# Storing turned groups from another queue, and turning the first batch's through DRAM as well

## The chip, the cores and the metric

The kernel runs on one core of a Trainium2 chip. The metric is the device time of one execution in microseconds. The time before is the median of three executions.

## The reference

Three stages are computed in float32, one after another, for 4 batches of 448 tokens:

```python
scores = scale * q @ k.T - log(S)          # 12 heads of 64, S = 448
x = sigmoid(scores) @ v                    # 1792 tokens x 768
g = (x @ w_a) * (x @ w_b)                  # 1792 x 1536
y = g @ w_out                              # 1792 x 768
logits = y @ phi                           # 1792 x 32
d = softmax(logits, over tokens)
slot_input = d.T @ y                       # 32 x 768, 8 experts of 4 rows
slot_out[e] = relu(slot_input[e] @ w1[e]) @ w2[e]
out = softmax(logits, over slots) @ slot_out
```

`w1` and `w2` are 25 MB each. The softmax over tokens runs over all 1792 tokens, so the experts can begin only after the last batch.

## The kernel before

The kernel keeps `g` transposed: `gT[b, fc]` is a tile of 128 features by 448 tokens, with 12 tiles (`fc`) for each batch `b`. It never forms `y`: it folds `w_out @ phi` into `wphi` for the logits, and computes `(d.T @ g) @ w_out` for the slots. For `d.T @ g` the tiles must be turned so that tokens lie on partitions. `group(b, gi)` turns four tiles at a time (three groups to a batch), and `dg` multiplies the turned groups by the softmax weights, adding up in `acc`.

The order of the work is written out by hand, with generators. `ab(0)` multiplies the first batch by `w_a` and `w_b` on TensorE (12 blocks of 36 matmuls), each matmul in three rounded parts. Between its steps the attention of the second batch goes on, VectorE, ScalarE and GpSimd convert the raw weights (`stage0`, `stage1`: loads at L330 and L333, converted weights stored to DRAM at L370), and `fill_step` moves one step of the waiting list `fill`, in which the groups stand. Batches 1 and 2 are computed together in `unit` with fewer products. `ab(3)` then does the last batch; its weights come back from DRAM by `load_w` (L454), are rounded on VectorE (L462) and GpSimd (L463), and are multiplied at L568. Only two half tiles of the buffer `wr` serve the last loads, so a load may start when the GpSimd instruction that reads its half is done. While `ab(3)` runs, `pump` (L982) loads the first expert weights into tiles that are free. The last group and logits (`last_LG`) follow, and then the experts, whose weights stream through the ring of tiles.

There are two ways to turn a group:

- by TensorE, in 16 transposes of 128x128 (L532) whose results are copied from PSUM alternately by ScalarE and VectorE (L534). All of batch 0, and the group `gi == 2` of the others, go that way.
- by VectorE, in four instructions that transpose blocks of 32x32 (L515). `store_gk` writes the half-turned tile to the DRAM buffer `gk32` in four transfers of 224 KB (L549), and `reload_gk` reads it back in the order that `dg` needs, in two transfers (L554, L555). The groups 0 and 1 of batches 1, 2 and 3 go that way.

All these transfers are issued on the queue of SyncE (SP), which takes its instructions in order and stops at one whose inputs are not there. For batch 3 the two turned tiles are kept in the list `turned_3` and stored together at step 57 of the 72 of `ab(3)`; steps 63 and 65 reload them. ScalarE's part in `ab(3)` is one copy out of PSUM for each block (L575); it also issues two small stores of logits (L852).

Of the kernel before, what the change touches and what calls it, by code (L numbers as in the profile page):

```python
# [9 lines left out]
F32 = mybir.dt.float32  # L10
# [8 lines left out]
B, H, S, D = 4, 12, 448, 64  # L19
# [16 lines left out]
def body(ctx, tc, q, k, v, w_a, w_b, w_out, phi, w1, w2, out):  # L36
    nc = tc.nc
    pe, act, dve, pool, sp = nc.tensor, nc.scalar, nc.vector, nc.gpsimd, nc.sync
# [12 lines left out]
    drp = ctx.enter_context(tc.tile_pool(name="drp", bufs=1, space=bass.MemoryType.DRAM))  # L51
# [12 lines left out]
    def ms(shape=(128, S)):  # L64
        tags = banks[run["banks"]]
        tag = tags[run["ms"] % len(tags)]
        run["ms"] += 1
        return ps_tile(tag, list(shape), 4 if tag == "sc" else 2)
# [8 lines left out]
    gk_01 = lgp.tile([128, 2, 2048], F32, name="gk_01")  # L77
# [11 lines left out]
    ab32 = drp.tile([KF, 2, 128, KD * 128], F32, name="ab32")  # L89
    out32 = drp.tile([128, KF, DM], F32, name="out32")  # L90
    clog32 = drp.tile([T, C, B, NS], F32, name="clog32")
    gk32 = drp.tile([B - 1, 2, S, 512], F32, name="gk32")

    idj = ident.rearrange("p (j s) -> p j s", j=4)
    small = gk_01.rearrange("p a n -> p (a n)")
# [204 lines left out]
    def att_to(cost):  # L300

        while att_state[0] < cost:
            n = next(att_g, None)
            if n is None:
                return
            att_state[0] += n

    def att_pairs(n):

        while (n - 1) not in xt:  # L310
            att_state[0] += next(att_g)
# [176 lines left out]
    def project(b, gi, n):  # L488

        t, r = ms(), 32 * n  # L490
        for j in range(n):
            fc = 4 * gi + j
            pe.matmul(t[32 * j:32 * j + 32], wphi[:, fc], gT[b, fc], start=True, stop=True)  # L493
        if gi == 0:
            act.copy(lp[b], t)
        else:
            dve.tensor_tensor(lp[b][:r], lp[b][:r], t[:r], op=ALU.add)

    def group(b, gi, evac=(act.copy, dve.tensor_copy) * 2):

        if (b, gi) != (B - 1, 2):
            for _ in range(GDEL):
                yield
        if (b, gi) != (B - 1, 2):
            project(b, gi, 4)
        if (b, gi) == (B - 1, 2):
            gk = e2.tile([128, 2048], F32, tag="e20", name="gk_3")
        elif b in (1, 2):
            gk = gk_01[:, b - 1]
        else:  # L510
            gk = gk_01[:, gi] if gi < 2 else gk_2
        if b and gi < 2:
            turned = gk[:, :4 * S].rearrange("p (n f) -> p n f", f=128)
            for j in range(4):
                dve.transpose(turned[:, :, 32 * j:32 * j + 32], gT[b, 4 * gi + j].rearrange("p (n t) -> p n t", t=32))  # L515
                yield
                if b < B - 1:
                    yield
                gT.pop((b, 4 * gi + j))
                live.discard(b * KF + 4 * gi + j)  # L520
            if b < B - 1:
                store_gk(b, gi, turned)
            else:
                turned_3.append(turned)
            return
        gk = gk.rearrange("p (c n) -> p c n", c=C)
        if gi == 2 and not b:
            yield
        for c in range(C):
            tp = ms((128, 512))  # L530
            for i in range(4):
                pe.transpose(tp[:, i * 128:(i + 1) * 128],  # L532
                             gT[b, 4 * gi + i][:, STARTS[c]:STARTS[c] + 128], ident)
            evac[c](gk[:, c], tp)  # L534
            if c != 1 or (b, gi) == (B - 1, 2):
                yield
                if b < B - 1 and c < C - 1:
                    yield
        for i in range(4):
            gT.pop((b, 4 * gi + i))  # L540
            live.discard(b * KF + 4 * gi + i)
        gtok[b, gi] = gk

    turned_3 = []

    def store_gk(b, gi, turned):
        dst = gk32[b - 1, gi].rearrange("(n t) (r f) -> r t n f", t=32, r=4)
        for r in range(4):
            sp.dma_start(out=dst[r], in_=turned[32 * r:32 * r + 32])  # L549

    def reload_gk(b, gi, t):
        t = t.rearrange("p (c n) -> p c n", c=C)
        src = gk32[b - 1, gi]
        sp.dma_start(out=t[:, :3], in_=src[:384].rearrange("(c p) n -> p c n", c=3))  # L554
        sp.dma_start(out=t[64:, 3], in_=src[384:])  # L555
        gtok[b, gi] = t
# [261 lines left out]
    def tokens(src, dst):  # L818

        t = ms((T, C, NS))  # L820
        for c in range(C):
            pe.transpose(t[:, c], src[:NS, c * T:(c + 1) * T], ident[:NS, :NS])
        dve.tensor_copy(dst, t)

    def weights(d, dst):
        t = ms((128, C, NS))
        for c in range(C):
            pe.transpose(t[:, c], d[:NS, STARTS[c]:STARTS[c] + 128], ident[:NS, :NS])
        dve.tensor_copy(dst, t)

    def dg(b, dtok, gp, groups):

        kept = not b or groups[0] == 2
        gk = gtok[b, groups[0]][:, None] if len(groups) == 1 else gk_01.rearrange("p g (c n) -> p g c n", c=C)
        o = gp.rearrange("p (g n) -> p g n", g=3)[:, groups[0]:groups[-1] + 1]
        for c in range(C):
            rows = slice(64 * (c == C - 1), 128)
            for j in range(4):
                pe.matmul(o[32 * j:32 * j + 32], dtok[rows, c], gk[rows, :, c, j * 128:(j + 1) * 128] if kept  # L839
                          else gk[rows, 0, c].rearrange("p (r j f) -> p j r f", r=4, j=4)[:, j],  # L840
                          start=(c == 0), stop=(c == C - 1))

    def LG(b):
        t = run["lsd2"]
        run["lsd"] = t[:, :S], t[:, S:2 * S]
        dtok, ltok = (t[:, i:i + C * NS].rearrange("p (c s) -> p c s", c=C) for i in (2 * S, 2 * S + C * NS))
        yield
        yield from logits(b)
        run["lg"] = b
        yield  # L850
        tokens(run["lsd"][0], ltok[:T])
        (act if b else sp).dma_start(out=clog32[:, :, b], in_=ltok[:T])  # L852
        yield
        weights(run["lsd"][1], dtok)
        for _ in range(4 if b == 1 else 1):
            yield
        gp = ms((128, FF // 4))
        for groups in ((0,), (1,), (2,)) if b else ((0, 1), (2,)):
            dg(b, dtok, gp, groups)
        if b:  # L860
            dve.scalar_tensor_tensor(acc, acc, run["al"], gp, op0=ALU.mult, op1=ALU.add)
        else:
            dve.tensor_copy(acc, gp)
        yield
        if b == B - 3:
            open_slots(run["e1"], [2, 3])
        elif b == B - 2:
            run.pop("lsd2")
            open_slots(run["e1"], [1, 4, 5])
# [83 lines left out]
    def open_slots(pl, names):  # L953
        slots.extend((pl, f"{pl.name}{i}") for i in names)
# [52 lines left out]
        next(bg)  # L1007

    base = att_state[0]
    for frac in ab(0):  # L1010
        att_to(base + NP * PAIR * min(1.0, frac * 1.02))
    att_pairs(2 * NP)
    for kk in range(NP):
        xt.pop(kk)
# [44 lines left out]
    for i, frac in enumerate(ab(B - 1)):  # L1059
        fc = i // 6  # L1060
        if i < 6:
            fill_step()
        if i == 6:
            while fill:
                fill_step()
            cp_ctx.close()
            xb_ctx.close()
            e1 = run["e1"] = ctx.enter_context(tc.tile_pool(name="e1", bufs=1, side="right"))
            run["lsd2"] = e1.tile([128, 2048], F32, tag="e11", name="lsd2")
            run["wr"] = e1.tile([128, 2048], F32, tag="e10", name="wr")  # L1070
            load_w(LAST + 6)
            load_w(LAST + 7)
            for x in range(4):
                nm = f"e1{2 + x}"
                reload_gk(1 + x // 2, x % 2, e1.tile([128, 2048], F32, tag=nm, name=nm))
            open_slots(e1, range(6, NE1))
            fill.append(LG(1))
            fill.append(LG(2))
        elif i == 57:
            for gi, t in enumerate(turned_3):  # L1080
                store_gk(B - 1, gi, t)
        elif i in (63, 65):
            reload_gk(B - 1, (i - 63) // 2, gk_01[:, (i - 63) // 2])
        if i == 66:
            dve.tensor_copy(wphi[:, :4], wphi[:, KF - 1:].to_broadcast([128, 4, NS]))
        if i >= 12 and i % 3 == 0:
            pump()
# [20 lines left out]
    for what in order0:  # L1108
        i = what[1]
        h, n, f0 = (0, 4, 4 * i) if i < 3 else (1, 6, 6 * (i - 3))  # L1110
# [8 lines left out]
    for kk in range(0, KD, 2):  # L1119
        f = ms((128, 2, 256))  # L1120
# [22 lines left out]
    for kk in range(0, KE, 2):  # L1143
        f = ms((128, 2, 256))
# [37 lines left out]
    for h, (c0, w) in enumerate(COLS):  # L1182
# [4 lines left out]
        t = ms((128, w))  # L1187
        pe.matmul(t, selF.rearrange("p j s -> p (j s)"), s4[:, c0:c0 + w], start=True, stop=True)
        evac[h](s4r[:, c0:c0 + w], t)
        for c in range(C):  # L1190
            op = []
            for b in range(B):
# [3 lines left out]
                r = slice(32 * b, 32 * b + 32)  # L1196
# [32 lines left out]
```

## Time and profile before

| | |
|---|---|
| median of 3 executions | 688.71 us (687.13 to 690.76) |
| the profiled execution | 689.2 us |
| its span from the first instruction to the last | 687.4 us |
| TensorE (PE) busy | 642.6 us, 93% |
| VectorE (DVE) busy | 396.4 us, 58% |
| ScalarE (ACT) busy | 296.1 us, 43% |
| GpSimd (POOL) busy | 309.6 us, 45% |
| mean granted TensorE clock | 0.983 of full speed |
| HBM read / written | 124.53 MB / 25.34 MB |

The busy times are those of the whole span. `ab(0)` lies between about 55 and 214 us, `ab(3)` between about 457 and 573 us, and the experts begin at about 584 us. In the rows, SPq and ACTq are the queues on which these engines issue transfers. A row names what an instruction writes and reads: `gk<-gk` at L549 is a store of a turned tile, `wr<-ab` a load of weights for the last batch, `e<-in_moe_w` a load of expert weights. In brackets stands how long the engine was idle before, and what ended that.

### The profile page before, as it was taken

The numbers are of one execution on the slowest core, as the hardware profiler recorded it, in microseconds if no ns is written. First come the engines' busy times: TensorE is split into PE (matmuls) and PEld (weight loads), VectorE is DVE, ScalarE is ACT, GpSimd is POOL, SyncE is SP. The second block draws the span as 40 slices with busy tenths as digits, with TensorE's granted clock in tenths as the row PEclk, the third lists the DMA queues.
The fourth block names the chain that finished last, engine by engine and source line by source line (L and its number), as shares of the span: only waits on it lengthen the run. The fifth ranks groups of instructions, "written<-read, shape, count | busy, mean of one in ns | idle before, by whom it ended". The sixth has DMA issues, their size and how long they took to land.

```text
span 687.4 us, 10893 instructions
## 1 busy us (share of the span) xinstructions
PE 642.6 (93%) x4035; PEld 457.4 (67%) x4035; DVE 396.4 (58%) x561; ACT 296.1 (43%) x535; POOL 309.6 (45%) x236
## 2 busy tenths in 40 slices
PE   6999999999999899999999999999999968997683
PEld 4557778777676455578988988888879856442132
DVE  4676898899895468849887777744232312200022
ACT  4888779678663768863332322212100002110021
POOL 0243667667762219639996575533335422000000
PEclk9999999999999999999999999999999989999998
DMA  8998999989845356111124424233999898999998
GB/s 197 262 282 210 288 300 324 275 250 336 223 159 141 70 93 113 32 43 46 47 75 119 101 91 100 76 117 115 340 371 338 329 314 305 409 416 415 408 357 277
DMA packets 145620, 150.58 MB, mean 219 GB/s; under 512 B 81600, under 2 KB 122912, under 8 KB 142496
## 3 DMA queue, kind: packets, MB, share of 16 engines
q1 hardware_dynamic: 144640, 149.78, 69.6%
q8 instruction: 32, 0.52, 0.3%
q10 hardware_dynamic: 928, 0.11, 0.1%
q14 instruction: 20, 0.16, 0.1%
HBM read 124.53 MB, written 25.34 MB: 218 GB/s over the span
## 4 chain that ended last, share of the span: by engine, by line
PE 76%; DMA 13%; ACT 2%; DVE 2%; issue 2%; SPq 2%; POOL 1%; DVEq 0%; ACTq 0%
PE ab L568 23%; PE sc L748 15%; DMA e<-in_moe_w 8%; PE ab L748 8%; PE sc L208 6%; PE sc L221 5%; PE ms L221 4%; DMA wr<-ab 2%; PE ms L170 2%; DMA qn<-in_q 2%; PE ms L839 1%; PE ab L208 1%; DMA gkp<-in_moe_w 1%; PE ms L493 1%; SPq L549 1%
## 5 line engine op out<-in xcount | busy, mean ns | idle before, releaser
L367 POOL TENSOR_TENSOR w<-gk,cy 128x768 int32<-128x768 int32 x36 | 66.2, 1838 | 91.9 <-DVE gk L362 56.2
L211 ACT ACTIVATE a<-sc,sums 112x448 f32<-112x448 f32 x147 | 84.4, 644 | 13.0 <-PE sc L208 12.8
L568 PE MATMUL ab<-t,wh 128*128 128x448 f32 x288 | 67.3, 380 | 5.6 <-DVE wh L462 5.6
L568 PEld LDWEIGHTS ab<-t,wh 128*128 128x128 f32 x288 | 54.9, 194 | 12.3 <-issue 7.3
L463 POOL TENSOR_TENSOR wl<-wr,wh 128x768 fp32r<-128x768 f32 x16 | 29.4, 1839 | 56.6 <-DVE wh L462 32.5
L575 ACT COPY misc<-ab 128x448 f32<-128x448 f32 x24 | 12.8, 535 | 88.7 <-PE ab L568 88.7
L463 POOL TENSOR_TENSOR wl<-w,wh 128x768 fp32r<-128x768 f32 x24 | 45.5, 1899 | 2.5 <-ACT wh L462 2.5
L1160 PE MATMUL ab<-e,gk 128*32 128x384 f32 x240 | 33.4, 530 | 10.1 <-DMA e<-in_moe_w 10.1
L360 DVE TENSOR_SCALAR mf<-gk 128x768 f32<-128x768 f32 x36 | 34.0, 945 | 13.3 <-ACT gk L349 13.3
L221 PE MATMUL sc<-a,vn 112*64 112x448 f32 x192 | 39.1, 546 | 1.0 <-ACT a L211 1.0
L221 PE MATMUL ms<-a,vn 112*64 112x448 f32 x192 | 38.7, 545 | 0.5 <-ACT a L211 0.5
L578 DVE TENSOR_TENSOR misc<-misc,ab 128x448 f32<-128x448 f32 x24 | 14.8, 615 | 36.9 <-PE ab L568 36.9
L208 PE MATMUL sc<-qh,kh 64*112 64x448 f32 x147 | 34.8, 424 | 0.7 <-ACT qh L158 0.6
L361 DVE TENSOR_SCALAR gk<-mf 128x768 uint32<-128x768 uint32 x36 | 34.3, 953 | 1.2
L568 PE MATMUL ab<-xh,wh 128*128 128x448 f32 x144 | 34.9, 377 | 0.0
L568 PE MATMUL ab<-xl,wh 128*128 128x448 f32 x144 | 34.5, 375 | 0.0
L568 PE MATMUL ab<-xh,wl 128*128 128x448 f32 x144 | 34.4, 374 | 0.0
L568 PE MATMUL ab<-t,wl 128*128 128x448 f32 x144 | 34.3, 373 | 0.0
L632 POOL TENSOR_TENSOR wx<-wr,wx 128x384 fp32r<-128x384 f32 x29 | 32.3, 1116 | 3.5 <-ACT wx L631 3.4
L631 ACT CAST wx<-T 128x384 fp32r<-128x384 f32 x21 | 10.8, 513 | 53.5 <-DVE T L653 33.9
L632 POOL TENSOR_TENSOR wx<-T,wx 128x384 fp32r<-128x384 f32 x23 | 24.8, 1080 | 17.0 <-ACT wx L631 15.7
L1199 DVE COPY o<-sc 112x384 f32<-112x384 f32 x11 | 5.6, 550 | 45.7 <-PE sc L1197 45.6
(458 smaller groups left out, 1521.3 us busy)
## 6 DMA issues: line engine op xcount, KB each, us to landing
e<-in_moe_w SPq DMA_DIRECT2D x23, 1024.0 KB, 7.8
e<-in_moe_w SPq DMA_DIRECT2D x23, 768.0 KB, 15.1
wr<-ab SPq DMA_DIRECT2D x14, 768.0 KB, 4.4
ab<-w SPq DMA_DIRECT2D x24, 384.0 KB, 7.2
vn<-in_v SPq DMA_DIRECT2D x24, 224.0 KB, 4.0
gk<-gk SPq DMA_DIRECT2D x24, 224.0 KB, 4.2
e<-in_moe_w SPq DMA_DIRECT2D x14, 384.0 KB, 8.6
wr_cv<-in_moe_w_a SPq DMA_DIRECT2D x6, 768.0 KB, 7.4
```

The source lines that it names most:

```text
L208: pe.matmul(sc[h], kx[r, cs], qx[r], start=(i == 0), stop=(i == 2))
L211: act.activation(a, sc[h], AF.Sigmoid, bias=nlog[:T], scale=1.0 / math.sqrt(D))
L221: pe.matmul(pv_t[g][64 * h:64 * h + 64], qkv_t["v", g][:, h, c, :], a_t.pop((g, h, c)), start=(c == 0), stop=(c == C - 1))
L360: dve.tensor_scalar(mf, m, LOW, HIGH, op0=ALU.max, op1=ALU.min)
L361: dve.tensor_scalar(mi, mf.bitcast(U32), 3, 0x3FFFFFFF, op0=ALU.logical_shift_left, op1=ALU.bitwise_and)
L367: pool.tensor_tensor(thirds(w), m.bitcast(I32), thirds(cy_t.pop(x)), op=ALU.add)
L463: pool.tensor_tensor(wl, t, wh.bitcast(F32), op=ALU.subtract)
L568: pe.matmul(t, w[:, kk * 128:(kk + 1) * 128], xt[b * NP + kk][xi], start=(s == 0 and kk == 0), stop=(s == 2 and kk == KD - 1))
L578: dve.tensor_tensor(g, g, t, op=ALU.mult)
L632: pool.tensor_tensor(w[:, 1], t, w[:, 0].bitcast(F32), op=ALU.subtract)
L748: pe.matmul(t, w[:, wi, k * 128:(k + 1) * 128], xs[ORDER[m], k][xi], start=(s == 0 and k == 0), stop=(s == 2 and k == 2))
L1160: pe.matmul(sps[h][32 * j:32 * j + 32], hT[:, 2 * x + i, 2 * j + g], ring[order2[n + j]][0][:, i, c0:c0 + w], start=(g == 0 and x == 0 and ...
```

## The change

Two things are changed, and a third follows from them.

- Batch 3: the stores of a turned group are issued by ScalarE, right after the group has been turned, with one `yield` (one call of `fill_step`) behind each. The list `turned_3` and the stores at step 57 on SP are gone. The reloads stay on SP at steps 63 and 65.
- Batch 0: its groups 0 and 1 are turned by VectorE, stored by SP as soon as they are turned, and reloaded by SP at steps 54 and 71 of `ab(0)`. Their 32 transposes on TensorE and 8 copies out of PSUM are gone.
- `dg` multiplies batch 0's groups one at a time, each with 16 matmuls of 128 columns, as it does for the other batches. Before, the first two went together with 256 columns.

```diff
@@ group(b, gi)
-        if b and gi < 2:
+        if gi < 2:
             turned = gk[:, :4 * S].rearrange("p (n f) -> p n f", f=128)
...
-            if b < B - 1:
-                store_gk(b, gi, turned)
-            else:
-                turned_3.append(turned)
+            yield from store_gk(b, gi, turned)
             return
...
     def store_gk(b, gi, turned):
-        dst = gk32[b - 1, gi].rearrange("(n t) (r f) -> r t n f", t=32, r=4)
+        dst = gk32[b, gi].rearrange("(n t) (r f) -> r t n f", t=32, r=4)
         for r in range(4):
-            sp.dma_start(out=dst[r], in_=turned[32 * r:32 * r + 32])
+            (act if b == B - 1 else sp).dma_start(out=dst[r], in_=turned[32 * r:32 * r + 32])
+            if b == B - 1:
+                yield
@@ dg
-        kept = not b or groups[0] == 2
+        kept = groups[0] == 2
@@ LG(b)
-        for groups in ((0,), (1,), (2,)) if b else ((0, 1), (2,)):
+        for groups in ((0,), (1,), (2,)):
@@ the loop over ab(0)
-    for frac in ab(0):
+    for i, frac in enumerate(ab(0)):
         att_to(base + NP * PAIR * min(1.0, frac * 1.02))
+        if i in (54, 71):
+            reload_gk(0, i // 60, gk_01[:, i // 60])
@@ the loop over ab(B - 1)
-        elif i == 57:
-            for gi, t in enumerate(turned_3):
-                store_gk(B - 1, gi, t)
```

The first place where the instructions move is SP's queue in the second half of `ab(3)`, from one load of expert weights (tile e14) to the reloads. Before:

```order
L982 DMA e14_5721<-in_moe2_w1 128x2048
L454 DMA wr_5115<-ab32_99 128x768
L549 DMA gk32_102<-gk_01_93 32x14x128 x8
L982 DMA e15_5756<-in_moe2_w1 128x2048
L454 DMA wr_5115<-ab32_99 128x768
L982 DMA gkp0_5783<-in_moe2_w1 128x2048
L454 DMA wr_5115<-ab32_99 128x768
L554 DMA gk_01_93<-gk32_102 128x3x512
```

The same place in the changed kernel:

```order
L979 DMA e14_5714<-in_moe2_w1 128x2048
L454 DMA wr_5103<-ab32_99 128x768
L979 DMA e15_5744<-in_moe2_w1 128x2048
L454 DMA wr_5103<-ab32_99 128x768
L979 DMA gkp0_5771<-in_moe2_w1 128x2048
L454 DMA wr_5103<-ab32_99 128x768
L551 DMA gk_01_93<-gk32_102 128x3x512
```

The eight stores that stood ahead of the last two loads of weights (`wr`) have left this queue, and nothing else in it has moved.

The second place is ScalarE in `ab(3)`, with the semaphores that each instruction waits for (DMAHW is that of an earlier transfer). Before there were only the copies out of PSUM here; the changed kernel has:

```order
L544 DMA gk32_102<-gk_01_93 32x14x128 [waits DMAHW2_49,DVE_49]
L572 COPY misc_95<-ab_5477 128x448 [waits PE_49]
L544 DMA gk32_102<-gk_01_93 32x14x128 [waits DMAHW5_49]
L544 DMA gk32_102<-gk_01_93 32x14x128 [waits DMAHW0_49]
L544 DMA gk32_102<-gk_01_93 32x14x128 [waits DMAHW2_49]
L572 COPY misc_95<-ab_5536 128x448 [waits PE_49]
L572 COPY misc_95<-ab_5590 128x448 [waits PE_49]
L572 COPY misc_95<-ab_5643 128x448 [waits PE_49]
L544 DMA gk32_102<-gk_01_93 32x14x128 [waits DMAHW2_49,DVE_49]
L544 DMA gk32_102<-gk_01_93 32x14x128 [waits DMAHW4_49]
L544 DMA gk32_102<-gk_01_93 32x14x128 [waits DMAHW6_49]
L572 COPY misc_95<-ab_5707 128x448 [waits PE_49]
```

Seven of the eight stores are in these rows; up to three now stand between two copies, and each waits for an earlier transfer to land.

The third place is VectorE in `ab(0)`, where the first group of batch 0 is turned (`mf` and `gk_2` are the conversion of the raw weights). Before:

```order
L534 COPY gk_01_93<-ms_1469 128x512
L578 TENSOR_TENSOR misc_95<-misc_95,ab_1441 128x448
L158 CAST kh_1505<-ms_1495 128x448
L159 TENSOR_TENSOR kl_1506<-ms_1495,kh_1505 128x448
L360 TENSOR_SCALAR mf_1516<-gk_2_94 128x768
L361 TENSOR_SCALAR gk_2_94<-mf_1516 128x3x256
L362 SCALAR_TENSOR_TENSOR gk_2_94<-wr_cv_98,gk_2_94 128x3x256
L534 COPY gk_01_93<-ms_1556 128x512
```

In the changed kernel:

```order
L515 STREAM_TRANSPOSE gk_01_93<-misc_95 128x14x32
L575 TENSOR_TENSOR misc_95<-misc_95,ab_1436 128x448
L158 CAST kh_1489<-ms_1479 128x448
L159 TENSOR_TENSOR kl_1490<-ms_1479,kh_1489 128x448
L360 TENSOR_SCALAR mf_1500<-gk_2_94 128x768
L361 TENSOR_SCALAR gk_2_94<-mf_1500 128x3x256
L362 SCALAR_TENSOR_TENSOR gk_2_94<-wr_cv_98,gk_2_94 128x3x256
L515 STREAM_TRANSPOSE gk_01_93<-misc_95 128x14x32
```

Transposes stand where the copies stood, and two more of them lie outside these rows, so that each of the two groups has four instead of two.

## Rows read from the trace of the kernel before

**Rows 1.** Chain of work that ended last, 537 to 580 us: start, us, what.

```profile
547.43 1.25 SPq L549
...
555.45 7.08 DMA wr<-ab
```

**Rows 2.** Timeline of all engines, 545 to 571 us: start, us, instruction, idle before.

```profile
546.44 7.42 SPq L549 DMA_DIRECT2D gk<-gk  x8
546.63 0.53 ACT L575 COPY misc<-ab 128x448 f32<-128x448 f32 x1 [6.91 <-PE ab L568]
...
547.42 1.85 POOL L463 TENSOR_TENSOR wl<-wr,wh 128x768 fp32r<-128x768 f32 x1 [1.39 <-DVE wh L462]
...
551.64 1.83 POOL L463 TENSOR_TENSOR wl<-wr,wh 128x768 fp32r<-128x768 f32 x1 [2.37 <-DVE wh L462]
...
553.87 2.64 PE L568 MATMUL ab<-t,wh 128*128 128x448 f32 x12
...
555.45 0.80 SPq L454 DMA_DIRECT2D wr<-ab  x1
...
556.35 1.40 PE L568 MATMUL ab<-t,wl 128*128 128x448 f32 x6
556.86 1.41 SPq L454 DMA_DIRECT2D wr<-ab  x1
...
562.64 0.56 DVE L462 CAST wh<-wr 128x768 fp32r<-128x768 f32 x1 [11.14 <-DMA wr<-ab]
...
563.35 4.82 PE L568 MATMUL ab<-t,wh 128*128 128x448 f32 x12 [5.60 <-DVE wh L462]
566.46 0.56 DVE L462 CAST wh<-wr 128x768 fp32r<-128x768 f32 x1 [2.72 <-DMA wr<-ab]
```

**Rows 3.** Windows: us, busy of PE, PEld, DVE, ACT, POOL, PEclk, DMA share, GB/s.

```profile
510.00:520.00 10.00, 10.00 (x50) 9.08 (x49) 4.14 (x6) 0.53 (x1) 3.69 (x2) 1.00 0.79 301
540.00:590.00 50.00, 41.80 (x307) 32.37 (x307) 10.71 (x25) 5.41 (x12) 13.83 (x19) 0.93 0.90 308
563.00:568.00 5.00, 4.65 (x13) 4.15 (x14) 1.43 (x4) 0.00 (x0) 2.68 (x2) 0.50 1.03 360
590.00:650.00 60.00, 50.44 (x386) 19.00 (x385) 5.85 (x10) 4.10 (x7) 0.00 (x0) 0.94 1.02 416
```

**Rows 4.** Issues of DMA, 500 to 600 us: count, KB each, median us to landing.

```profile
e<-in_moe_w SPq DMA_DIRECT2D x23, 1024.0 KB, 7.8
wr<-ab SPq DMA_DIRECT2D x8, 384.0 KB, 4.9
```

**Rows 5.** Timeline of VectorE, 511 to 516 us, the first turned group's last transpose.

```profile
513.68 0.63 DVE L515 STREAM_TRANSPOSE gk<-misc 128x448 f32<-128x448 f32 x1
```

**Rows 6.** Timeline of TensorE in the first product, 109 to 130 us.

```profile
117.28 1.03 PE L532 MATMUL ms<-ident,misc 128*128 128x128 f32 x8
118.07 1.46 PE L568 MATMUL ab<-xh,wl 128*128 128x448 f32 x6
```

**Rows 7.** Waits of TensorE, 100 to 213 us: us in total, times, longest.

```profile
PE ms L532 <- ACT wT L393: 0.5, 2, 0.2
PE ms L532 <- DVE kl L159: 0.3, 1, 0.3
```

**Rows 8.** Chain of work that ended last, 237 to 243 and 484 to 506 us: `dg`.

```profile
238.55 3.14 PE ms L839 x64
...
485.97 3.43 PE ms L839 x96
```

**Rows 9.** Lines L515 and L534: ns of one, shortest/median/longest.

```profile
L515 DVE STREAM_TRANSPOSE gk<-misc x16: 600/632/639, 358.0 to 540.4; 128x448 f32<-128x448 f32 x16
L534 DVE COPY gk<-ms x10: 681/690/693, 120.9 to 472.0; 128x512 f32<-128x512 f32 x10
```

**Rows 10.** Windows, columns as in rows 3, the first product's busiest stretch on VectorE.

```profile
150.00:180.00 30.00, 29.25 (x178) 21.95 (x177) 28.31 (x31) 21.51 (x34) 21.91 (x12) 1.00 0.98 314
```

**Rows 11.** Waits of SP's queue, 100 to 200 us: us in total, times, longest.

```profile
SPq L330 <- DVE gk L362: 10.9, 4, 3.7
```

More of the change, by code (lines that the diff above doesn't have):

```diff
@@ L91, in body @@
     clog32 = drp.tile([T, C, B, NS], F32, name="clog32")
-    gk32 = drp.tile([B - 1, 2, S, 512], F32, name="gk32")
+    gk32 = drp.tile([B, 2, S, 512], F32, name="gk32")
     idj = ident.rearrange("p (j s) -> p j s", j=4)
@@ L542, in group @@
         gtok[b, gi] = gk
-    turned_3 = []
     def store_gk(b, gi, turned):
-        dst = gk32[b - 1, gi].rearrange("(n t) (r f) -> r t n f", t=32, r=4)
+        dst = gk32[b, gi].rearrange("(n t) (r f) -> r t n f", t=32, r=4)
         for r in range(4):
-            sp.dma_start(out=dst[r], in_=turned[32 * r:32 * r + 32])
+            (act if b == B - 1 else sp).dma_start(out=dst[r], in_=turned[32 * r:32 * r + 32])
+            if b == B - 1:
+                yield
     def reload_gk(b, gi, t):
         t = t.rearrange("p (c n) -> p c n", c=C)
-        src = gk32[b - 1, gi]
+        src = gk32[b, gi]
         sp.dma_start(out=t[:, :3], in_=src[:384].rearrange("(c p) n -> p c n", c=3))
```

## The prediction

> **What bounds the kernel now.** I read the chain of waits first. It is TensorE's work nearly everywhere, and the place where it leaves TensorE late in the last batch's product is the one that this change touches: there it runs through the stores of the turned groups on SP's queue and then through one load of weights [rows 1]. The timeline of that stretch says how. SP begins the eight stores at 546.44 and is busy with them for 7.42 us. The half tile that the next load needs is free when GpSimd's subtraction ends, at 547.42 + 1.85 = 549.27; the load is issued at 555.45, 6.2 us late. The one after it could start at 551.64 + 1.83 = 553.47 and is issued at 556.86, 3.4 us late. The weights of the first are rounded only at 562.64. TensorE has used up what it had at 556.35 + 1.40 = 557.75 and starts again at 563.35, after 5.60 us with nothing to do [rows 2]. When it does start, its granted clock is 0.50 of full speed, the 1.2 GHz level, until about 568 [rows 3]: the same twelve matmuls take 4.82 us where they took 2.64 just before [rows 2].
>
> The windows behind that place say whether time saved there is saved at the end. From 590 to 650 the DMA engines are busy throughout and move 416 GB/s: this is the stream of expert weights, bound by bandwidth, and it starts when TensorE has used the first of the loaded tiles. Between 540 and 590 their share is 0.90 [rows 3].
>
> For the first batch I read TensorE's timeline in the first product and then the engines that could hold it up. TensorE goes from one matmul to the next with waits of some 0.3 us, and VectorE is busy for 28.31 of 30 us in the tightest stretch [rows 6, 7, 10].
>
> **A. The last batch's stores leave SP's queue.** Gone is the wait of 5.60 us. Gone with it is the slow clock behind it, 4.82 - 2.64 = 2.18 us, since TensorE went into the wait at full speed and fell only there. Together 7.78 us.
>
> Does something else hold the two loads? If they take as long to land as before, the first is rounded at 549.27 + (562.64 - 555.45) + 0.56 = 557.02, ahead of the 557.75 at which TensorE wants it. The second took 566.46 - 556.86 = 9.60 us; it would be ready at 553.47 + 9.60 + 0.56 = 563.63. TensorE wants it one block of 18 matmuls later, at 557.75 + (557.75 - 553.87) = 561.63, so it would wait 2.0 us. With the median of these loads, 4.9 us, it is there at 558.9 [rows 2, 4]. The slow landings of before came behind eight stores and two loads of 1 MB issued in a burst; the changed queue spreads these, so I take the median and keep the 2.0 us as a bound.
>
> The stores themselves go on. ScalarE issues them, at 7.42 / 8 = 0.93 us each if SP's row holds for it. It has 6.91 us free before each copy [rows 2], so three stores between two copies, 2.8 us, delay nobody, as long as they wait for nothing. The bytes still have to move: the DMA engines have 50 x (1 - 0.90) = 5.0 us free between 540 and 590. The first group is turned by 513.68 + 0.63 = 514.31, and its four stores move there, to a stretch of 10 us with a share of 0.79, 2.1 us free [rows 3, 5]. So the transfers let TensorE come forward by 5.0 + 2.1 = 7.1 us before the loads fall behind. Of 7.78 and 7.1 I take the smaller: **A gives 7.1 us**, between 3.0 (only the 5.0 us, less the 2.0) and 7.8. The experts then start 7.1 us earlier with the same bytes to stream, so the end moves as much.
>
> **B. The first batch's two groups go by VectorE and DRAM.** TensorE loses 32 transposes. Eight of them take 118.07 - 117.28 = 0.79 us from start to start, so 32 take 3.2 us [rows 6]. Their waits for a PSUM bank, 0.5 and 0.3 us, go as well [rows 7]: 4.0 us, half of it in each group. The duration of one is longer than its share of this, since they overlap. The Trainium skill (TensorE: Matmul & The Clock Gate, Part 4: PE-mode transpose) gives about 275 ns for one transpose inside a kernel; by that figure 32 would be worth 8.8 us, while the trace shows 0.10 us from one to the next, so the trace decides.
>
> `dg` of the first batch takes the shape of the others: 3.43 instead of 3.14 us, +0.3 [rows 8].
>
> VectorE gets 8 transposes of 0.632 us and loses 4 copies of 0.690: 5.06 - 2.76 = +2.3 us, 1.15 for each group [rows 9]. ScalarE loses four copies. For the first group's share VectorE's waits in the timeline have room. The second group is turned in the stretch from 150 to 180, where VectorE is free for 1.7 us; with 1.15 us more it can be pressed by only 0.5 us, so I credit the second group with 0.5 us instead of 2.0 [rows 10]. **B gives 2.0 + 0.5 - 0.3 = 2.2 us**, between +3.7 (all of the 4.0) and -2.6 (VectorE's 2.3 us on the path and no gain).
>
> The eight new stores and four reloads on SP: the first group's stores stand right ahead of a load of raw weights (L330), before which SP waits for VectorE anyway, up to 3.7 us at a time [rows 11]. Four issues of 0.93 us are 3.7 us, so the load is late by about nothing and by 3.7 us at most. I count it as nothing: raw tiles are loaded four jobs ahead. The second group's stores and the reloads lie where no raw load follows soon.
>
> **Sum.** 7.1 + 2.2 = 9.3 us. The profiled execution took 689.2 us (span 687.4): 679.9. It lies 0.5 us above the median shown, 688.71, so I predict **679.4 us** for the median.
>
> **The rivals.** A difference of less than 0.5%, 3.4 us, is about what a measurement of this kernel cannot tell from none.
>
> *VectorE becomes the bound in the first product.* For it: 28.31 of 30 us busy [rows 10]. Against it: the wait that TensorE has for it is 0.3 us in all [rows 7], and it is this full only where the raw weights are converted. Then B costs 2.6, and the time is 688.7 - 7.1 + 2.6 = 684.2. Chance 0.13.
>
> *The transfers keep most of A.* The loads fall behind since the engines have 5.0 us free and no more, and the second load is 2.0 us late: A gives 3.0, and the time is 688.7 - 3.0 - 2.2 = 683.5. For it: the landings of 7.2 and 9.6 us; against it: the median of 4.9. Chance 0.09. The Trainium skill (DMA: Bandwidth & Descriptors, Issuing engines are not separate DMA queues) speaks for it: transfers from several engines share the same 16 DMA engines, and another issuer saves only the issuing time, usually small beside the transfer. By that rule this rival's time is the one to expect; the trace agrees in so far as it shows the DMA engines nearly full, but the time lost on SP was 6.2 us of issuing.
>
> *The change does not take the wait away.* SP's loads wait for transfers some places back, which now include ScalarE's stores; if these come late, the loads are as late as before. A gives nothing and B its 2.2: 686.5. Chance 0.08.
>
> *ScalarE stops at its stores: slower.* Each store waits for an earlier transfer, and ScalarE's copies behind it free the PSUM bank that TensorE needs. If that transfer is a load of 1 MB still under way, 7.8 us to landing [rows 4], three stores between two copies take 3 x (7.8 + 0.93) = 26.2 us, of which 6.91 are free: TensorE stands for 19.3 us, and the time is 679.4 + 19.3 = 698.7. It decides where three stores take longer than 6.91 us together, and is slower than before where they take more than some 16. Against it: the transfers waited for were issued several places earlier. Chance 0.06.
>
> **How the numbers follow.** The forecast has 0.64. Its own range is 7.8 + 3.7 = 11.5 us of gain at most, 677.2, and a microsecond of spread as the runs before show: 676.0. Upwards the range takes in the two rivals at 684.2 and 683.5 with as much spread: 685.5. That leaves out the last two, 0.14. Faster by over 0.5% (under 685.3) is the forecast with the first two rivals, 0.86, less 0.03 for their edge: 0.83. Within 0.5%: 0.08 + 0.03 = 0.11. Slower: 0.06.
>
> **What would show it.** Right: no wait of TensorE for a load of weights in the second half of the last batch's product, and a clock of 1.00 through it; the last two loads issued within about a microsecond of GpSimd's end; the experts' stream starting some 9 us earlier and as long as before. For B: the first product 2 to 3 us shorter. Wrong: ScalarE's stores with waits of several microseconds ahead of its copies; TensorE waiting for the last load; in the first product, TensorE waiting for VectorE for more than a microsecond, or for raw weights, or a DMA share there that makes loads land later.

## The result and the profile after

The changed kernel takes **681.75 us** (median of 4 runs, 679.84 to 683.6) where the kernel before takes 689.72 beside it: ratio 0.9891, 95% interval 0.9853 to 0.9928. Run again beside the last experiments it took 680.65 against 689.51, ratio 0.9862 (0.9828 to 0.9895). That is 7.5 and 9.5 us of gain by the ratios; the forecast was 9.3. The profiled execution of the changed kernel is the slowest of its four, 683.6 us with a span of 681.8, so small shifts between the two traces are read from experiments and not from it alone. Product `ab` is L565 in the changed kernel (L568 before), the turned groups' stores are L544 (L549).

The chain that ended last, changed kernel, through the second half of the last batch's product (start, us, what), answers to [rows 1]:

```profile
539.72 27.47 PE ab L565 x132
567.19 0.88 PE ms L493 x6
```

One unbroken piece of TensorE's work where the chain left it for SP's stores and a load of weights. The timeline of the stretch, start, us and instruction, idle before in brackets, answers to [rows 2]:

```profile
543.07 2.15 ACTq L544 DMA_DIRECT2D gk<-gk  x3
548.63 0.53 ACT L572 COPY misc<-ab 128x448 f32<-128x448 f32 x1 [6.90 <-PE ab L565]
548.63 0.31 ACTq L544 DMA_DIRECT2D gk<-gk  x1
...
550.41 1.84 POOL L463 TENSOR_TENSOR wl<-wr,wh 128x768 fp32r<-128x768 f32 x1 [2.38 <-DVE wh L462]
...
552.27 0.33 SPq L454 DMA_DIRECT2D wr<-ab  x1
...
554.72 1.84 POOL L463 TENSOR_TENSOR wl<-wr,wh 128x768 fp32r<-128x768 f32 x1 [2.48 <-DVE wh L462]
555.87 2.64 PE L565 MATMUL ab<-t,wh 128*128 128x448 f32 x12
...
557.06 0.33 SPq L454 DMA_DIRECT2D wr<-ab  x1
557.82 0.56 DVE L462 CAST wh<-wr 128x768 fp32r<-128x768 f32 x1 [3.23 <-DMA wr<-ab]
...
561.78 0.56 DVE L462 CAST wh<-wr 128x768 fp32r<-128x768 f32 x1 [1.30 <-DMA wr<-ab]
```

The load that was 6.2 us late is issued at 552.27, when GpSimd's subtraction ends (550.41 + 1.84 = 552.25). The next is 0.5 us behind its own (554.72 + 1.84 = 556.56, issued 557.06), where it was 3.4 us late. TensorE's twelve matmuls take 2.64 us throughout. The windows, columns as in [rows 3]:

```profile
540.00:590.00 50.00, 47.40 (x361) 35.55 (x363) 16.68 (x36) 7.76 (x16) 13.85 (x19) 1.00 0.98 364
590.00:650.00 60.00, 47.50 (x366) 16.68 (x362) 2.08 (x3) 2.30 (x4) 0.00 (x0) 0.93 1.02 412
```

Between 540 and 590 the clock is 1.00 instead of 0.93, and the DMA engines' share is 0.98 instead of 0.90: 1 us of their time is left idle where 5.0 were. From 590 on the stream of expert weights runs as before.

The first product did not get shorter. From the start of its first matmul to the start of its last it took 158.1 us before (55.4 to 213.5) and takes 159.0 here, 158.2 in the repeated run. The experts begin 5.9 us earlier than before, at 578.4 instead of 584.4 (8.1 us earlier in the repeated run), where some 9 us were forecast. TensorE's waits in the first product (us in total, times, longest; before they were 1.8 us in all):

```profile
PE ms L170 <- ACT wT L393: 2.8, 3, 2.2
PE ms L392 <- POOL w L367: 0.9, 1, 0.9
PE ms L392 <- DVE wphi L418: 0.9, 1, 0.9
PE ms L493 <- ACT wT L393: 0.2, 1, 0.2
```

The chain of the changed kernel leads there. L367 is GpSimd's last step of converting a tile of raw weights; it writes one of three buffers (`w32`), and L370 stores that to DRAM (`out<-w`, `ab<-w`) on SP's queue:

```profile
152.08 8.98 DMA out<-w
...
161.22 1.84 POOL w L367
...
163.08 0.95 ACT gk L349
164.03 0.80 ACT cy L353
164.82 1.82 ACT a L211 x4
...
166.79 0.46 ACT wT L393
...
167.30 0.76 PE ms L170 x4
```

A store of converted weights takes 8.98 us; GpSimd waits for its buffer; ScalarE's copies that TensorE needs stand behind the conversion; TensorE's work resumes at 167.30. The length of that store is not the whole cause: the same chain has one of 8.95 us at 122.55, ahead of any store of a group. Ahead of the chain's second store, SP's queue had issued the first group's stores (`137.22 4.15 SPq L544 DMA_DIRECT2D gk<-gk x4`), and the DMA engines' share from 140 to 160 is 0.97, against 0.89 before (0.92 in the repeated run). SP's queue behind them shows the next three stores of converted weights. Before:

```profile
140.40 0.33 SPq L330 DMA_DIRECT2D wr_all<-in_moe_w_out  x1
140.82 0.38 SPq L370 DMA_DIRECT2D ab<-w  x1
...
148.24 0.64 SPq L370 DMA_DIRECT2D ab<-w  x1
...
149.93 0.69 SPq L370 DMA_DIRECT2D out<-w  x1
```

In the changed kernel:

```profile
141.48 1.84 SPq L330 DMA_DIRECT2D wr_all<-in_moe_w_out  x1
143.41 1.24 SPq L370 DMA_DIRECT2D ab<-w  x1
...
150.68 0.81 SPq L370 DMA_DIRECT2D ab<-w  x1
...
152.08 0.93 SPq L370 DMA_DIRECT2D out<-w  x1
```

GpSimd had finished these three at 137.73, 142.41 and 146.45 before, and at 138.18, 142.89 and 146.89 in the changed kernel. So they are issued 3.1, 5.8 and 3.5 us after it before, and 5.2, 7.8 and 5.2 us after it now, some 2 us later each. From issue to landing they take 7.9, 6.6 and 7.9 us before, and 8.2, 6.7 and 9.0 now. GpSimd's waits for stores in the first product were `ab<-w` 4.2 us before; now:

```profile
POOL w L367 <- DMA out<-w: 6.7, 4, 2.5
POOL w L367 <- DMA ab<-w: 1.8, 1, 1.8
```

And the windows of the stretch, changed kernel (before, TensorE was busy for 19.25 us of the second one, at 1.00):

```profile
140.00:160.00 20.00, 20.00 (x121) 15.08 (x118) 14.86 (x18) 12.17 (x20) 12.24 (x6) 1.00 0.97 287
160.00:180.00 20.00, 15.94 (x85) 10.66 (x83) 16.90 (x21) 15.58 (x24) 14.40 (x8) 0.91 0.87 276
168.00:170.00 2.00, 2.00 (x7) 1.54 (x6) 1.25 (x2) 0.38 (x1) 2.00 (x2) 0.50 1.06 396
```

Behind TensorE's waits, which end at 167.30, its granted clock falls to 0.50, the 1.2 GHz level: the first product loses by the waits and by slow matmuls behind them.

So the traces suggest that A gave nearly all of the gain, and that B's gain was given back by its own stores. The experiments test that.

### The profile page after: what moved, and what is told of

Same layout as the page of the kernel before. It is cut to its first block, busy times and chain, and to the rows that moved or that the text cites. A ratio compares the mean times of both kernels' runs of the same rounds, so it can differ in the third digit from the quotient of the medians.

```text
span 681.8 us, 10900 instructions
## 1 busy us (share of the span) xinstructions
PE 639.4 (94%) x4035; PEld 455.0 (67%) x4035; DVE 397.3 (58%) x565; ACT 294.0 (43%) x531; POOL 311.8 (46%) x236
## 4 chain that ended last, share of the span: by engine, by line
PE 77%; DMA 13%; ACT 3%; DVE 2%; issue 2%; POOL 1%; SPq 0%; DVEq 0%; ACTq 0%; POOLq 0%
PE ab L565 24%; PE sc L745 15%; DMA e<-in_moe_w 8%; PE ab L745 8%; PE sc L208 6%; PE sc L221 5%; PE ms L221 4%; DMA out<-w 3%; PE ms L170 2%; PE ms L836 2%; PE ab L208 1%; PE ms L493 1%; ACT a L211 1%; DMA gkp<-in_moe_w 1%; PE sc L1193 1%
## 5 line engine op out<-in xcount | busy, mean ns | idle before, releaser
L367 POOL TENSOR_TENSOR w<-gk,cy 128x768 int32<-128x768 int32 x36 | 66.7, 1853 | 91.1 <-DVE gk L362 57.6
L565 PE MATMUL ab<-t,wh 128*128 128x448 f32 x288 | 65.1, 371 | 0.0
L565 PEld LDWEIGHTS ab<-t,wh 128*128 128x128 f32 x288 | 53.4, 188 | 6.1 <-issue 1.3
L463 POOL TENSOR_TENSOR wl<-w,wh 128x768 fp32r<-128x768 f32 x24 | 47.0, 1960 | 2.5 <-ACT wh L462 2.5
L565 PE MATMUL ab<-xh,wl 128*128 128x448 f32 x144 | 35.4, 383 | 0.0
L565 PE MATMUL ab<-xh,wh 128*128 128x448 f32 x144 | 34.9, 378 | 0.0
L565 PE MATMUL ab<-xl,wh 128*128 128x448 f32 x144 | 34.5, 375 | 0.0
L565 PE MATMUL ab<-t,wl 128*128 128x448 f32 x144 | 34.3, 373 | 0.0
```

What stands on the lines that cost most here:

```text
L367: pool.tensor_tensor(thirds(w), m.bitcast(I32), thirds(cy_t.pop(x)), op=ALU.add)
L463: pool.tensor_tensor(wl, t, wh.bitcast(F32), op=ALU.subtract)
L565: pe.matmul(t, w[:, kk * 128:(kk + 1) * 128], xt[b * NP + kk][xi], start=(s == 0 and kk == 0), stop=(s == 2 and kk == KD - 1))
```

## The experiments

Each is compared with the kernel before, run beside it on the same chip. The three values of before belong to three such sets: A alone, B alone and the two without transfers; A's two halves, the fourth buffer and the later stores, each alone; and the rest. Kernels of different sets are compared by their ratios. "First" and "last" are the lengths of the first and the last batch's product in the profiled execution, from the start of the first matmul to the start of the last.

| kernel | median us | ratio, 95% | first | last |
|---|---|---|---|---|
| before | 688.93, 689.52, 689.51 | 1 | 158.1 | 115.1 |
| changed | 681.75; again 680.65 | 0.9891; 0.9862 | 159.0; 158.2 | 107.1; 107.1 |
| A alone | 682.30 | 0.9894 (0.9875 to 0.9913) | 157.2 | 107.2 |
| B alone | 688.31 | 0.9991 (0.9976 to 1.0007) | 157.2 | 114.4 |
| A's moment, SP's queue | 683.92 | 0.9931 (0.9909 to 0.9954) | 157.5 | 108.3 |
| A's queue, old moment | 687.37 | 0.9963 (0.9949 to 0.9977) | 158.4 | 111.3 |
| no transfers in B | 677.88 | 0.9840 (0.9823 to 0.9857) | 154.1 | 107.2 |
| no transposes either | 677.07 | 0.9832 (0.9811 to 0.9854) | 154.0 | 107.1 |
| changed, 4 buffers | 675.56 | 0.9815 (0.9793 to 0.9838) | 153.6 | 107.1 |
| A alone, 4 buffers | 681.19 | 0.9869 (0.9844 to 0.9893) | 157.4 | 107.1 |
| changed, later stores | 677.31 | 0.9817 (0.9793 to 0.9841) | 152.9 | 107.1 |
| later stores, 4 buffers | 677.46 | 0.9812 (0.9789 to 0.9834) | 152.9 | 107.1 |
| B's stores on ScalarE | 690.70 | 1.0016 (0.9993 to 1.0039) | 167.1 | 107.1 |

**1. A alone.** The kernel before with the last batch's stores from ScalarE's queue as each group is turned (the list `turned_3` and the stores at step 57 are gone):

```diff
-            if b < B - 1:
-                store_gk(b, gi, turned)
-            else:
-                turned_3.append(turned)
+            yield from store_gk(b, gi, turned)
...
-            sp.dma_start(out=dst[r], in_=turned[32 * r:32 * r + 32])
+            (act if b == B - 1 else sp).dma_start(out=dst[r], in_=turned[32 * r:32 * r + 32])
+            if b == B - 1:
+                yield
```

> The last batch's stores go to ScalarE as they are turned; the first batch is turned by TensorE as before. Theory 1 (the stores on ScalarE give all of the gain, and the first batch's way through DRAM gives none or costs a little): 680 to 681.5 us, the changed kernel's time or better, 8 us under before. Theory 2 (each part gives what was forecast, and the wait of some 4 us that the changed kernel's trace shows in the first product belongs to that execution): 684 us, some 2 us over the changed kernel. In both TensorE has no wait for a load of weights in the last batch's product.

682.30 us, between the two theories: 7.3 us by the ratio (6.0 to 8.6). The last product is 7.9 us shorter, and in it no load of weights is waited for: TensorE's only wait from 515 to 576 us is the 1.0 us below, behind the product (whose last matmul starts at 565.6).

```profile
PE sc L825 <- ACT misc L802: 1.0, 1, 1.0
```

**2. B alone.** The changed kernel with the last batch as before (`turned_3`, step 57, SP's queue); the first batch's two groups go by VectorE and DRAM.

```diff
-            yield from store_gk(b, gi, turned)
+            if b < B - 1:
+                store_gk(b, gi, turned)
+            else:
+                turned_3.append(turned)
...
-            (act if b == B - 1 else sp).dma_start(out=dst[r], in_=turned[32 * r:32 * r + 32])
-            if b == B - 1:
-                yield
+            sp.dma_start(out=dst[r], in_=turned[32 * r:32 * r + 32])
...
+        elif i == 57:
+            for gi, t in enumerate(turned_3):
+                store_gk(B - 1, gi, t)
```

> The first batch's two groups go by VectorE and DRAM; the last batch's stores stay on SP at step 57. Theory 1: 689 to 691 us, no gain against before or a loss of up to 1 us, with TensorE waiting in the first product between 155 and 185 us behind GpSimd's conversion. Theory 2: 687 us, 2 us under before. In both the wait of 5.6 us in the last batch's product is there as before.

0.9991: not to be told from nothing, 0.6 us by the ratio, where 2.2 was forecast. The wait in the last product is there as before, 5.5 us. With A's 7.3 the 0.6 makes up the whole change, within the noise.

**3. Which half of A works?** First the new moment with the old queue, then the new queue with the old moment, both against the kernel before and without B:

```diff
-            if b < B - 1:
-                store_gk(b, gi, turned)
-            else:
-                turned_3.append(turned)
+            yield from store_gk(b, gi, turned)
...
             sp.dma_start(out=dst[r], in_=turned[32 * r:32 * r + 32])
+            if b == B - 1:
+                yield
...
-        elif i == 57:
-            for gi, t in enumerate(turned_3):
-                store_gk(B - 1, gi, t)
```
```diff
-            sp.dma_start(out=dst[r], in_=turned[32 * r:32 * r + 32])
+            (act if b == B - 1 else sp).dma_start(out=dst[r], in_=turned[32 * r:32 * r + 32])
```

> Only the moment is changed: the last batch's stores stay on SP's queue, but are issued one by one as each group is turned; the first batch as before. If the moment is what counts (eight stores in a burst just ahead of the two tightest loads), the wait of TensorE in the last batch's product is gone and the time is some 682 us, as with the stores on ScalarE. If the queue is what counts (any store ahead of a load of weights delays it), the last product still has a wait of 1 to 4 us for a load of weights, and the time is 684 to 687 us.

> Only the queue is changed: the last batch's eight stores are issued together at step 57, but by ScalarE; the first batch as before. If the queue is what counts, some 682 us: SP's loads go out on time, and ScalarE's 7.4 us of issuing just about fit between two of its copies. If the moment counts, the stores in a burst still make the last two loads land late: TensorE waits 2 to 5 us and the time is 684 to 687 us.

The moment alone gives 4.8 us, the queue alone 2.5, both 7.3; the intervals of the moment alone and of both just touch (0.9909 and 0.9913). Stores spread along SP's queue delay loads a little (TensorE waits 0.9 us for a rounded tile). Eight stores at once on ScalarE's queue show why the queue alone is not enough, in that kernel's timeline and chain:

```profile
547.09 12.99 ACTq L549 DMA_DIRECT2D gk<-gk  x8
...
560.12 0.53 ACT L575 COPY misc<-ab 128x448 f32<-128x448 f32 x1 [12.50 <-DMA wr<-ab]
...
560.71 4.26 PE L568 MATMUL ab<-t,wh 128*128 128x448 f32 x12 [2.50 <-ACT misc L575]
```
```profile
547.09 9.04 DMA gk<-gk
556.13 0.02 SPq L454
...
556.18 3.57 DMA wr<-ab
...
559.77 0.31 ACTq L549
```

ScalarE is held for 12.99 us, its copy comes at 560.12, and TensorE waits 2.50 us for it. The chain shows each queue waiting for the other's transfers: SP's load for ScalarE's first store, ScalarE's last store for that load. This is the forecast's slower rival in small. The Trainium skill (DMA: Bandwidth & Descriptors, Issuing engines are not separate DMA queues) holds that another issuer saves only the issuing time, usually small beside the transfer. The queue alone, with 2.5 us, does not contradict that, but it is a net figure: SP's loads no longer stood behind the stores, and TensorE waited for ScalarE instead. The larger part of A's gain came with another moment.

**4. What do B's transfers cost, and what its transposes on VectorE?** The changed kernel without the first batch's eight stores and four reloads; VectorE's transposes stay, and the tiles are used half-turned. In the second kernel the eight transposes are gone too, and zeros stand in the tiles.

```diff
+        pool.memset(gk_01[:, :, 4 * S:], 0.0)
...
-            yield from store_gk(b, gi, turned)
+            if b:
+                yield from store_gk(b, gi, turned)
+            else:
+                gtok[b, gi] = gk.rearrange("p (c n) -> p c n", c=C)
...
-        if i in (54, 71):
-            reload_gk(0, i // 60, gk_01[:, i // 60])
+        pass
```
```diff
+        pool.memset(gk_01, 0.0)
...
-                dve.transpose(turned[:, :, 32 * j:32 * j + 32], gT[b, 4 * gi + j].rearrange("p (n t) -> p n t", t=32))
+                if b:
+                    dve.transpose(turned[:, :, 32 * j:32 * j + 32], gT[b, 4 * gi + j].rearrange("p (n t) -> p n t", t=32))
```

> The changed kernel without the first batch's 8 stores and 4 reloads: its two groups are turned by VectorE and used as they lie (that part of the sums is left out of place; 256 columns of each tile are set to zero at the start). Theory 1 (the transfers are what costs in the first product, since they hold up the stores of the converted weights): 678 us, 3 to 4 us under the changed kernel, and no wait of GpSimd for such a store beyond what before has. Rival (VectorE's 2.3 us more are what costs): 681 us, as the changed kernel.

> As the run without transfers, and the 8 transposes on VectorE are left out too: the first batch's two groups are not turned at all (zeros stand in their place). If the transfers are what costs, the time is within 1 us of the run without transfers; if VectorE's time costs, it is 2 us or more under it. It shows what TensorE's 32 transposes are worth at most: forecast 3.7 us, so some 677 to 678 us.

Without the transfers the first product is 154.1 us, 4.0 shorter than before, and the ratio to before falls by 0.9894 - 0.9840 = 0.0054 below A alone: 3.7 us, the upper bound that the forecast gave for B. All its runs (676.85 to 679.08) lie below all of the changed kernel's (679.55 to 683.6). VectorE's transposes cost some 0.6 us (0.9840 against 0.9832), and the intervals overlap. So the transfers take the gain back, and nothing that can be told goes to VectorE.

**5. How do they take it?** If through the three buffers of converted weights, a fourth gives it back with every byte and the order of all issues left as they are:

```diff
-        w = cvp.tile([128, 768], I32, tag="w32", name="w32", bufs=3)
+        w = cvp.tile([128, 768], I32, tag="w32", name="w32", bufs=4)
```

> The changed kernel with four instead of three buffers for the converted weights (w32), which GpSimd writes, and which come free when their store to DRAM has landed. If the first batch's transfers cost because they make these stores land late and GpSimd waits for a buffer, the wait is gone and most of the 3.9 us come back: 678 to 679 us. If they cost because SP issues the loads of raw weights late (four stores of some 1 us stand ahead of one), or in another way, 681 to 682 us.

675.56 us, 0.9815: below the expected 678 to 679, and faster than both kernels (all its runs, 675.15 to 678.22, lie below all eight of the changed kernel's, 679.55 to 683.6), and the first product is 153.6 us although SP's four stores still take as long (`135.82 4.82 SPq L544 DMA_DIRECT2D gk<-gk x4`) and the DMA engines are as full. GpSimd's waits, the two largest, and the windows to set beside those of the changed kernel:

```profile
POOL w L367 <- DVE gk L362: 32.3, 18, 8.1
POOL A11l L657 <- DMA gk<-gk: 9.5, 1, 9.5
```
```profile
140.00:160.00 20.00, 20.00 (x117) 15.38 (x116) 18.63 (x20) 14.90 (x23) 14.67 (x9) 1.00 0.99 276
160.00:180.00 20.00, 19.18 (x117) 13.77 (x117) 19.47 (x25) 15.17 (x25) 14.27 (x8) 1.00 0.94 313
```

No wait of L367 for a store is left, and TensorE is busy for 19.18 us of the second window, at 1.00, where it had 15.94 at 0.91. The stores themselves are still late: the three that the changed kernel issued 5.2, 7.8 and 5.2 us after GpSimd go out 5.5, 7.8 and 5.1 us after it here. So the buffer does not make them earlier, it makes their lateness harmless. The 9.5 us are a new wait behind the product, for the group's reload; TensorE has 1.2 us of waiting there. The control is the fourth buffer without B:

> The first part of the change alone, as in the earlier run of it (682.3 us, ratio 0.9894), with four buffers for the converted weights instead of three; the second part is left out. Theory: the fourth buffer gives back what the first batch's new stores cost, so without them it has little to give back: 681 to 682.5 us, ratio 0.987 to 0.990, first product 156 to 157.5 us as without it. Rival: three buffers were short already, with or without the new stores, and the fourth buffer is a gain of its own that has nothing to do with the second part: about 678 us, ratio 0.983 to 0.985, first product near 154 us; the second part would then be worth only the 2 to 3 us between this run and the changed kernel with four buffers (675.56).

0.9869 against 0.9894 for A alone, 1.7 us with overlapping intervals, and a first product of 157.4 against 157.2: without B's stores the buffer buys nothing that can be told, although GpSimd's waits for stores fall there too, from 8.4 us to 1.1. With them it gives 3.2 to 5.2 us, most of which is thus B's; whether a part is a gain of its own is not shown. With four buffers on both sides B is worth 0.0054, 3.7 us, and the two intervals (0.9793 to 0.9838, 0.9844 to 0.9893) do not overlap.

The 8.4 us also say what not to read. A alone has as much waiting of GpSimd for stores as the changed kernel (6.7 + 1.8 = 8.5 us), and TensorE waits there for only 1.4 us in the first product, against 4.8. The sum of GpSimd's waits does not show the loss; what counts is whether a late conversion holds one of ScalarE's copies long enough for TensorE. In the three traces that lose (the changed kernel twice, B alone) TensorE waits 2.2 us for that copy between 162 and 168 us, and its clock between 160 and 180 is 0.91. (In B alone the trace puts GpSimd's wait just ahead of it down to TensorE and not to a store, so there the way through a buffer is argued.) Without transfers, with four buffers and with later stores that wait is 1.5, 0.8 and at most 0.2 us, and the clock is 1.00.

**6. The other cure: store later.** The first group's four stores are held back to step 60 of the first product, and both groups are reloaded at its end; alone, and with the fourth buffer:

```diff
-            yield from store_gk(b, gi, turned)
+            if b or gi:
+                yield from store_gk(b, gi, turned)
+            else:
+                held.append(turned)
...
-        if i in (54, 71):
-            reload_gk(0, i // 60, gk_01[:, i // 60])
+        if i == 60:
+            for _ in store_gk(0, 0, held.pop()):
+                pass
+        elif i == 71:
+            for gi in range(2):
+                reload_gk(0, gi, gk_01[:, gi])
```

> The changed kernel with the first group's four stores of the first batch moved from its turning (about 137 us) to step 60 of the first product (about 187 us), where the raw weights have been loaded, and its reload from step 54 to 71. Either way of costing (SP's time, or full DMA engines) is then avoided for this group: 678 to 679 us, and the first product 155 us long. If the cost lies with the second group or the reloads, it stays at 681 to 682 us.

> The changed kernel with both cures: the first group's stores of the first batch held back to step 60, and four buffers for the converted weights. Theory: both cure the same wait (GpSimd for a buffer whose store is late), so together they give no more than either alone: 674.5 to 677 us, ratio 0.980 to 0.983, first product 152 to 153.5 us. Rival: they cure two different losses (the buffer, and SP's 4 us at its stores) and add up: 672 to 673.5 us, ratio 0.975 to 0.977, first product near 150 us.

0.9817 and 0.9812, first product 152.9 in both: either cure is enough, and they do not add up. They remove the same loss: with the fourth buffer there, moving SP's issues and the bytes out of the full stretch gains nothing more that can be told.

**7. B's stores on ScalarE's queue**, to part SP's issuing from the bytes:

```diff
-            (act if b == B - 1 else sp).dma_start(out=dst[r], in_=turned[32 * r:32 * r + 32])
+            (act if b in (0, B - 1) else sp).dma_start(out=dst[r], in_=turned[32 * r:32 * r + 32])
```

> The changed kernel with the first batch's eight stores issued from ScalarE's queue instead of SP's, at the same places; bytes and moments stay. Theory: what the stores cost is their share of the DMA engines' time while these are nearly full, so the queue doesn't matter: 680.5 to 683 us, ratio 0.987 to 0.991, first product 157 to 160 us and GpSimd still waiting for its buffer's store. Rival: what they cost is SP's 4.15 us at issuing, behind which weights' loads and stores stand: about 678 us, ratio 0.983 to 0.985, first product near 154 us. Third: ScalarE, which the first product needs for its copies, is held at the issues: slower than the changed kernel, 684 us and over, with TensorE waiting for ScalarE's copies.

690.70 us, as the third expectation said (684 and over): all of A's gain is lost. The timeline of ScalarE and TensorE there:

```profile
137.11 3.89 ACTq L544 DMA_DIRECT2D gk<-gk  x2
...
141.04 0.86 ACT L393 COPY wT<-ms 128x384 f32<-128x384 f32 x2 [3.60 <-DMA ab<-w]
...
141.57 1.01 PE L170 MATMUL ms<-ident,qn 112*128 112x112 f32 x4 [4.08 <-ACT wT L393]
...
200.81 0.31 ACTq L544 DMA_DIRECT2D gk<-gk  x1
201.16 0.86 ACT L393 COPY wT<-ms 128x384 f32<-128x384 f32 x2 [6.36 <-DMA gk<-gk]
...
201.69 1.01 PE L170 MATMUL ms<-ident,qn 112*128 112x112 f32 x4 [6.28 <-ACT wT L393]
```

The last store of each group stands still until an earlier transfer has landed, and ScalarE's copies for TensorE stand behind it: TensorE waits 4.08 and 6.28 us, and the first product takes 167.1 us. Because ScalarE stops, the run does not part SP's issuing from the bytes.

**8. The changed kernel again**, unedited.

> The changed kernel once more, nothing edited, beside the same runs of the kernel before as the other kernels of this call. Theory: the second part adds nothing to the first, so it lies at the first part's own result: 681 to 683 us, ratio 0.988 to 0.991. Rival: its first runs were a little slow and the second part does give 1 to 3 us: 679 to 681 us, ratio 0.985 to 0.988.

680.65 us, 0.9862: in the rival's range, but its interval (0.9828 to 0.9895) takes in A alone's 0.9894. Over both sets of runs B is worth 0.2 to 2.2 us on top of A; whether it is above zero with three buffers stays open.

## Why the prediction was right, and where it was not

**The forecast held**: 681.75 and 680.65 us lie in its range, 2.4 and 1.3 us over 679.4. About 1 us of that is the kernel before, which took 689.72 and 689.51 beside them instead of 688.71.

**A, 7.1 us: right, with its mechanism.** 7.3 us alone. The wait of 5.60 us and the slow clock behind it are both gone. The choice of the median landing was right: from the issue of the two loads to VectorE's rounding it is 557.82 - 552.27 = 5.6 and 561.78 - 557.06 = 4.7 us, against 7.2 and 9.6 in the burst of before. The cap of 7.1 us by idle DMA time is not borne out: the last product became 7.9 us shorter, as much as the whole 7.78, and the measured 7.3 (6.0 to 8.6) does not tell 7.1 and 7.78 apart. The share of 0.98 between 540 and 590 does not prove the cap either, as the window now holds more of the experts' stream, which begins at 578.4 instead of 584.4. The stretch from the experts' first matmul to the end is 103.0 us before and 103.4 after, so time saved ahead of it was saved at the end.

**ScalarE's stores: right for the places used.** Three between two copies took 2.15 us late in the product and 3.90 (`517.79 3.90 ACTq L544 DMA_DIRECT2D gk<-gk x3`) at its busiest place, where 2.8 was estimated and 6.91 were free. Experiments 3 and 7 show that the rival was real: eight in a row took 12.99 us, and in the first product four were too many.

**B, 2.2 us: measured 0.6 alone and 0.2 to 2.2 on top of A; that it is no further off is luck, by two errors that partly cancel.** TensorE's 4.0 us and `dg`'s 0.3 fit: without transfers B gives 3.7 us, and `dg` takes 3.43 us in the changed kernel (`240.21 3.43 PE ms L836 x96`). The credit of 0.5 instead of 2.0 us for the second group was wrong: 28.31 of 30 us busy on VectorE did not make it a bound, and its transposes cost 0.6 us, not told from nothing. **The step that failed is "The eight new stores and four reloads on SP": "I count it as nothing: raw tiles are loaded four jobs ahead."** It looked behind the stores for loads alone. The load was indeed late by only about a microsecond (141.48 instead of 140.40). But the transfers cost 0.9891 - 0.9840 or 0.9862 - 0.9840, that is 3.5 or 1.5 us, since stores of converted weights stand behind them on SP's queue and share the DMA engines: they go out some 2 us later, land late, and hold the three buffers that GpSimd writes. The forecast had read a DMA share of 0.98 there and asked only what VectorE would do; that GpSimd waits for such stores (4.2 us) was in the trace before, though that sum alone would not have told the loss. The sign that it had named for B, a first product 2 to 3 us shorter, did not come.

A small slip of the range: its ends lie 1.2 and 1.3 us beyond 677.2 and 684.2, not one. Nothing hangs on it.

In part open: whether SP's issuing or the bytes make those stores late. Experiments 5 and 6 show only that neither costs time once the buffer or the moment is changed. The rows of SP's queue put the larger part on issuing: some 2 us for each of the three stores, against 0.1 to 1.1 us more from issue to landing. But an issue is itself longer there (L330 took 1.84 us instead of 0.33), and what lengthens it, the queue or the bytes ahead of it, is not shown.

## What to carry to other kernels

When a store is put into a stretch with full DMA engines, look for the small pool whose buffers are released by other stores, and count how many it has: one buffer more, or a later moment, was worth 3 to 5 us here, while the same buffer without the new stores was worth 1.7 us, not told from nothing. Moving stores off a queue that issues loads paid most when the moment was moved too (7.3 us against 2.5), and it pays only if the engine that takes them has nothing urgent behind them: a queue that must wait at a store stops its engine's own work.

## What was not expected

- An issue is not a fixed price. Alone ScalarE's store took 0.31 us; three in a row 2.15 or 3.90; eight 12.99, where SP's eight had taken 7.42.
- Two queues can stop each other: SP's load of weights waited for ScalarE's store, and ScalarE's last store for that load (experiment 3).
- Stores of 384 KB took 8.95 and 8.98 us in the chain of the changed kernel, longer than the median of 6.9 that its page gives for `ab<-w`; the first of them was issued before any of the new stores.
